# Two small B and C loads, and the scaling and transposing that use them, moved ahead of the last quarter of the input weight

## The chip, the cores and the metric

The kernel runs on one core of one Trainium2 chip. The metric is the device time of one execution in microseconds (us). A core has five engines that run their own instruction streams in order: PE multiplies matrices, DVE, ACT and POOL work on vectors, and SP issues the transfers (DMAs) between the device memory and the core. An engine that meets an instruction whose input isn't there stands, and everything behind it in its stream stands too.

## What is computed

A state-space layer (Mamba2-SSD) over 4 batches, 8 heads and 768 positions, followed by a two-layer perceptron with a tanh GELU over its 3072 x 256 result.

```
for c in range(24):                       # reference: chunks of 32 positions
    cum = cumsum(log a);  L = exp(cum_i - cum_j) * causal
    y_intra = ((C B^T) * L) x
    y_inter = (C state) * exp(cum)
    state = exp(sum log a) * state + sum_j B_j x_j * decay_from_j
h = y.reshape(3072, 256) @ w_in           # w_in 256 x 2048
out = gelu_tanh(h) @ w_out                # w_out 2048 x 256
```

## The kernel before

The kernel takes chunks of Q = 128 positions, six for each batch, 24 in all, and treats two chunks with all 8 heads as a unit u (12 units, 0 to 11). Instead of the exponentials of differences it scales B by a running product of a (`rt0`, `rt`) and C by its reciprocal (`pt0`, `pt`), so that the decay between two positions is a product of the two; a triangle `tri` does the causal part.

Each piece of work is a step: a name, an engine and a function. What order the steps are recorded in, and so in which order each engine gets its instructions, stands written out by hand in the string ORDERED (line 17). An engine's stream is the steps of ORDERED that run on it, in that order; `:A`, `:D` or `:P` behind a name puts a step on ACT, DVE or POOL in place of its usual engine. The framework adds the waits that the data and the buffers need.

```
for w in ORDERED.split():
    ...
        name, _, e = w.partition(":")
        s = steps[name]
        s.eng, s.pre = e or s.eng, int(n or 0)
        s.fn()
```

The steps that the change and the prediction speak of are these.

- Loads on SP: load_wi.q (L192) is quarter q of w_in, 512 KB, 0 to 3. load_bc1.1 and load_bc1.0 (L156) are C and B of chunks 4 and 5 of the first batch, 128 KB each, in pieces of 128 bytes. load_wo.q (L196) is a quarter of w_out, load_x.u (L177, two transfers) x of a unit, load_bc.b.1 and load_bc.b.0 (L170) C and B of batch b.
- wi.q.k and wo.q.k (L339 on POOL, L337 on ACT, L341 on DVE) cast the halves of such a quarter to bf16.
- tp2 (L364) and recip1 (L397) make on DVE the scales for chunks 4 and 5. mul1.0 and mul1.1 (L459, POOL) scale B and C with them. T1.0 and T1.1 (L467, PE) transpose the results into the PSUM banks ga and gb. bh1 and ce1.0, ce1.1 (L478) copy them out. N1 (L487, PE) transposes B back, and bn1 copies that. tp6 (L364) and recip.b (L404) make the scales of the later batches, pe (L408, L409, DVE), pp (L415, PE) and pend (a copy) the decay at the ends of chunks.
- For unit u: G.u (L618, PE) is C B^T into ga and gb; M.u.0 and M.u.1 (L628, DVE) are the masked products from ga and gb; D.u (L651, PE) is the update of the state; S.c.. (L699) and SP.c (L706) carry the state on DVE; Y.u (L673 and L682, PE) is the layer's output, and yev.u copies it to xm as bf16. For units 0 and 1 x is already in the core and XX, XD and xn spread it; from unit 2 on castx.u casts it.
- s1.u.i (L732, PE, i = 0 to 7) multiplies two of the 16 column blocks of w_in with xm into one of the two PSUM buffers hp; gelu.u.i (L736, ACT) empties it. s1.u.4 and s1.u.5 use quarter 2 of w_in, s1.u.6 and s1.u.7 quarter 3. s2.c.q (L750, PE) multiplies with quarter q of w_out; oev.c copies the result out and store.c writes it.

The buffers hp are shared: D.u and pp take one as well, so a matmul into hp also waits until the copy or the gelu of the one but last user is done.

Of the kernel before, what the change touches and what calls it, by code (L numbers as in the profile page):

```python
# [19 lines left out]
recip0 c_m16 mulc.0 ~51 tw.1 ew.1.1:A mulc.1 tw.2 mulb c_sub c_unp c_ends ~4 tw.0 peq ew.0.2 ew.0.1  # L20
load_wi.1 ew.0.0:A ew.1.2 c_par ~4 G.0 x4.1 ew.1.0 x4.0:D M.0.0 ~4 ppq GE.2 GE.3 pendq XX.0 ME.2
XD.0 xn.1 ME.3 xn.0:D load_wi.2 SP.0 ~17 Y.0 wi.0.1:A wi.0.0:A S.0.0 clip R S.0.1 yev.0.0.2 wi.1.1
XX.1 XD.1 wi.1.0 tp2 wi.2.1 xn.2 s1.0.0 G.1 S.1.0 s1.0.1 xn.3 gelu.0.0 gelu.0.1 s1.0.2 gelu.0.2
M.1.1 wi.2.0 M.1.0 s1.0.3 gelu.0.3 s1.0.4 s1.0.5 recip1 S.1.1 gelu.0.4 gelu.0.5 SP.1 load_wi.3
wi.3.1 wi.3.0 load_bc1.1 s1.0.6 load_bc1.0 mul1.0:P SP.2 pe mul1.1:P T1.0 bh1:D tp6 Y.1 gelu.0.6 pp
load_wo.0 pend:D yev.1.0.2 T1.1 N1 wo.0.0 s1.0.7 load_x.2 ce1.1:D castx.2.None ce1.0:D recip.1
s1.1.0 bn1 SP.3 gelu.0.7 wo.0.1 G.2 D.2 gelu.1.0 S.2.0 s1.1.1 gelu.1.1 s2.0.0.0.o s1.1.2 gelu.1.2
s1.1.3 load_bc.1.1 SP.4 load_bc.1.0 M.2.1 M.2.0 gelu.1.3 load_wo.1 s2.0.1.0.o mul.1.0 s1.1.4
mul.1.1:P recip.2 load_x.3 gelu.1.4 wo.1.0 s1.1.5 wo.1.1 Y.2 gelu.1.5 castx.3.None s1.1.6 yev.2.0.2
T.1.0 s1.1.7 gelu.1.6 load_wo.2 E.1.0 T.1.1 s1.2.0 N.1 gelu.1.7 gelu.2.0 E.1.1 bn.1:D s1.2.1 F.1  # L30
s2.0.0.1.o wo.2.0 wo.2.1:D s1.2.2 gelu.2.1 s2.0.1.1.o D.3 G.3 S.3.0 gelu.2.2 s1.2.3 gelu.2.3 S.3.1
M.3.0 M.3.1 load_wo.3 load_x.4 wo.3.0:A s2.0.0.2.o s2.0.1.2.o wo.3.1 SP.6 s1.2.4 s1.2.5 castx.4.None
s2.0.0.3.o s2.0.1.3.o gelu.2.4 gelu.2.5 oev.0:D s1.2.6 Y.3 oev.1 yev.3.0.2:D s2.1.0.0.o s2.1.0.1.o
s2.1.0.2.o gelu.2.6 s2.1.0.3.o s1.2.7 S.4.0 oev.2 recip.3 S.4.1 s1.3.0 s2.1.1.0.o M.4.1 s2.1.1.1.o
gelu.3.0 s2.1.1.2.o gelu.2.7 s2.1.1.3.o s1.3.1 s1.3.2 gelu.3.1 gelu.3.2 oev.3:D s2.2.0.0.o
s2.2.0.1.o s1.3.3 gelu.3.3 s2.2.0.2.o load_bc.2.1 load_bc.2.0 s2.2.0.3.o mul.2.1:P s1.3.4 M.4.0
load_x.5 s1.3.5 gelu.3.4 mul.2.0:P castx.5.None:D SP.7 oev.4:D SP.8 SP.9 s2.2.1.0.o s2.2.1.1.o
gelu.3.5 s2.2.1.2.o s1.3.6 s2.2.1.3.o gelu.3.6 Y.4 load_wr.2.1 s1.3.7 oev.5:D s2.3.0.0.o yev.4.0.2
load_x.6 load_wr.2.0 S.5.0 gelu.3.7 s1.4.0 s2.3.0.1.o M.5.0 load_tr.2.1 gelu.4.0 SP.10 M.5.1 s1.4.1
s2.3.0.2.o castx.6.None s1.4.2 load_bn.2 gelu.4.1 load_tr.2.0 s1.4.3 store.0 s2.3.0.3.o gelu.4.2  # L40
# [961 lines left out]
```

## Time and profile before

| | |
|---|---|
| median of 3 runs | 117.01 us (116.45 to 117.2) |
| the profiled execution | 116.76 us |
| its span in the profile | 115.0 us |
| busy share of PE, DVE, ACT, POOL | 94%, 59%, 61%, 23% |
| matmuls of s1 (L732) | 384, 53.4 us busy, 273 ns each |
| gelu (L736) | 96, 54.3 us busy, 596 ns each |
| moved by DMA | 16.00 MB in 43103 packets |

Times in the profile count from the start of the span. A row of the timeline gives start, duration, engine, line, operation and tiles, how many instructions are taken together, and in brackets the engine's idle time before and what ended it. For transfers the duration is that of SP's issue, and the time to landing stands in the rows of the DMA view. A matmul's duration includes its way through the array: two of 273 ns can start 109 ns apart, so eight of one row take about 0.9 us of PE.

### The profile page before, as it was taken

To read this page: it belongs to the slowest core of one execution; us is meant where nothing else is said; L and a number is where in the kernel's file an instruction comes from. 1 tells how busy PE (TensorE), PEld (TensorE's weight loads), DVE (VectorE), ACT (ScalarE), POOL (GpSimd) and SP (SyncE) were. 2 spreads that over 40 slices of the span, in tenths; PEclk is the share of its full clock that TensorE was granted. 3 is DMA by queue.
4 is the path that set the end of the run, shared out by engine and by line. 5 is a ranking of instruction groups with operands and counts; after the bars stand their busy time and mean duration, and the time that the engine had idled before them with its cause. 6 is when DMAs were issued, how large, how long until landed. Compare 5 with 4: busy or idle time off the path is not lost.

```text
span 115.0 us, 3377 instructions
## 1 busy us (share of the span) xinstructions
PE 108.1 (94%) x1421; PEld 91.7 (80%) x1421; DVE 68.0 (59%) x136; ACT 70.0 (61%) x133; POOL 25.9 (23%) x54
## 2 busy tenths in 40 slices
PE   6979888999999999999999999999999999999990
PEld 2235566888879997989989899889898898999970
DVE  6889998989974755969448491186750851010100
ACT  3159687687654455747675876456495576758620
POOL 7636856806439020201120030000000000000000
PEclk9999999999999999999999999999999999999999
DMA  0999979979994779997556922350003020001113
GB/s 24 231 309 336 332 212 191 317 132 321 215 238 101 141 177 203 196 272 175 88 131 150 209 62 85 111 86 0 0 9 134 0 71 26 0 0 55 42 62 120
DMA packets 43103, 16.00 MB, mean 139 GB/s; under 512 B 36688, under 2 KB 41552, under 8 KB 43088
## 3 DMA queue, kind: packets, MB, share of 16 engines
q1 hardware_dynamic: 42896, 15.70, 55.3%
q8 instruction: 11, 0.18, 0.7%
q10 hardware_dynamic: 192, 0.09, 0.3%
q14 instruction: 4, 0.03, 0.1%
HBM read 11.07 MB, written 3.93 MB: 130 GB/s over the span
## 4 chain that ended last, share of the span: by engine, by line
PE 82%; DVE 5%; DMA 4%; SPq 3%; issue 2%; ACT 2%; DVEq 0%
PE hp L732 35%; PE o_ps L750 34%; DMA x_t<-in_x_dram 4%; PE yb L750 3%; PE yb L673 3%; PE ga L618 2%; PE yb L682 2%; DVE m L628 1%; DVE sp_new L706 1%; SPq L164 1%; ACT gT L736 1%; SPq L151 1%; SPq L160 1%; DVE rt L364 1%; DVE r_t L354 1%
## 5 line engine op out<-in xcount | busy, mean ns | idle before, releaser
L736 ACT ACTIVATE gT<-hp 128x512 bf16<-128x512 f32 x96 | 54.3, 596 | 28.9 <-PE hp L732 28.6
L732 PE MATMUL hp<-xm,w_in_sb 128*128 128x256 bf16 x384 | 53.4, 273 | 1.1 <-DVE s_new L699 0.5
L750 PE MATMUL o_ps<-w_out_sb,gT 128*128 128x256 bf16 x352 | 46.8, 273 | 0.0
L732 PEld LDWEIGHTS <-w_in_sb 128*128 128x128 bf16 x384 | 41.2, 114 | 4.0 <-issue 2.7
L750 PEld LDWEIGHTS <-gT 128*128 128x128 bf16 x384 | 37.4, 98 | 4.1 <-issue 0.4
L341 DVE COPY o_sb<-o_ps 128x256 f32<-128x256 f32 x12 | 5.1, 425 | 26.9 <-PE o_ps L750 26.9
L628 DVE TENSOR_TENSOR m<-ga,tri 128x1024 bf16<-128x1024 f32 x12 | 14.6, 1216 | 0.0
L628 DVE TENSOR_TENSOR m<-gb,tri 128x1024 bf16<-128x1024 f32 x11 | 13.4, 1216 | 0.0
L339 POOL CAST x<-x_t 128x512 bf16<-128x512 f32 x8 | 6.0, 756 | 28.1 <-DMA x_t<-in_x_dram 24.4
L706 DVE SCALAR_TENSOR_TENSOR sp_new<-s_new,pend,bmask 128x256 bf16<-128x256 f32 x17 | 8.0, 483 | 0.1
L699 DVE SCALAR_TENSOR_TENSOR s_new<-s_new,pend,hp 128x64 f32<-128x64 f32 x13 | 3.5, 272 | 7.4 <-PE hp L651 7.3
L720 PE MATMUL yb<-wz 128*128 128x512 bf16 (+2 forms) x21 | 6.6, 455 | 1.1 <-DVE warm L226 1.1
L337 ACT ACTIVATE o_sb<-o_ps 128x256 f32<-128x256 f32 x10 | 3.8, 383 | 5.1 <-PE o_ps L750 3.8
L682 PE MATMUL yb<-m,x 128*32 128x128 bf16 x192 | 6.1, 220 | 0.0
L337 ACT ACTIVATE xm<-yb 128x512 bf16<-128x512 f32 x8 | 4.8, 596 | 1.3 <-PE hp L651 0.7
L720 PEld LDWEIGHTS <-wz 128*128 128x128 bf16 x21 | 2.3, 116 | 4.1 <-issue 2.1
L673 PE MATMUL yb<-ce,sp_new 128*32 128x128 bf16 x160 | 5.3, 221 | 0.0
L339 POOL CAST w_out_sb<-wf 128x512 bf16<-128x512 f32 x6 | 4.1, 692 | 4.7 <-DMA wf<-in_moe_w_out_dram 4.7
L618 PE MATMUL ga<-ce,bh 32*128 32x256 bf16 x48 | 4.7, 273 | 0.3 <-DVE par L289 0.3
L618 PE MATMUL gb<-ce,bh 32*128 32x256 bf16 x48 | 4.7, 273 | 0.0
L750 PE MATMUL yb<-w_out_sb,gT 128*128 128x256 bf16 x32 | 4.5, 273 | 0.0
L682 PEld LDWEIGHTS <-x 128*32 128x32 bf16 x192 | 3.7, 96 | 0.9 <-issue 0.9
(114 smaller groups left out, 75.0 us busy)
## 6 DMA issues: line engine op xcount, KB each, us to landing
out_dram<-o_sb SPq DMA_DIRECT2D x24, 128.0 KB, 2.0
x_t<-in_x_dram SPq DMA_DIRECT2D x20, 128.0 KB, 3.9
wf<-in_moe_w_in_dram SPq DMA_DIRECT2D x4, 512.0 KB, 7.0
wf<-in_moe_w_out_dram SPq DMA_DIRECT2D x4, 512.0 KB, 7.1
bc_t<-in_C_dram SPq DMA_DIRECT2D x3, 384.0 KB, 4.7
bc_t<-in_B_dram SPq DMA_DIRECT2D x3, 384.0 KB, 5.7
scr<-bc SPq DMA_DIRECT2D x4, 192.0 KB, 2.3
x_t<-in_x_dram SPq DMA_DIRECT2D x1, 512.0 KB, 4.4
```

What stands on the lines that cost most here:

```text
L337: nc.scalar.activation(o, i, AF.Copy)
L339: nc.gpsimd.tensor_copy(out=o, in_=i)
L341: nc.vector.tensor_copy(out=o, in_=i)
L618: nc.tensor.matmul(out=gbank(g)[:, 256 * k:256 * k + 256], lhsT=bh_of(2 * u + k)[gs], rhs=ce_of(2 * u + k)[gs], start=True, stop=True, til ...
L628: nc.vector.tensor_tensor(out=m_of(u)[:, 2 * i:2 * i + 2].rearrange("p g k e t -> p (g k e) t"), in0=gx[i].rearrange("p g (k t) -> p (g k) ...
L673: nc.tensor.matmul(out=y4[32 * j:32 * j + 32, k, w], lhsT=sp[:, 32 * h:32 * h + 32], rhs=ce_of(gc)[:, h % 2], start=first(j), stop=False, ...
L682: nc.tensor.matmul(out=y4[32 * j:32 * j + 32, k, w], lhsT=X16[u][:, k, 32 * h:32 * h + 32], rhs=m[:, h // 2, h % 2, :], start=first(j), st ...
L706: nc.vector.scalar_tensor_tensor(out=sp_new.rearrange("p (g d) -> p g d", g=4), in0=(XN[0][:, H * D:H * D + 64] if gc == 0 else state[("s" ...
L720: nc.tensor.matmul(out=t[:, 0:m * 128], lhsT=wz, rhs=w3.to_broadcast([128, m, 128]), start=True, stop=True, skip_group_check=True)
L732: nc.tensor.matmul(out=hp[:, j * T:(j + 1) * T], lhsT=w_in_k[:, w, q, k], rhs=xm[:, w, u * T:(u + 1) * T], start=(w == 0), stop=(w == 1))
L736: nc.scalar.activation(gts[u][:, 2 * i:2 * i + 2], hps.pop((u, i)).rearrange("p (j t) -> p j t", j=2), AF.Gelu_apprx_tanh)
L750: nc.tensor.matmul(out=ops[gc], lhsT=gts[u][:, fi, k * Q:(k + 1) * Q], rhs=w_out_sb[:, fi, :], start=(fi == 0 and (u > 0 or k == 0)), stop ...
```

## The change

Only the string ORDERED is changed; no function is touched. In SP's stream load_bc1.0 and load_bc1.1, B now ahead of C, come in front of load_wi.3 in place of behind it. On POOL mul1.0 comes in front of the two casts of quarter 3, and mul1.1 stays behind them. On PE T1.0 comes between s1.0.3 and s1.0.4; Y.1 and pp come in front of s1.0.6; T1.1 and N1 come between s1.0.6 and s1.0.7; s2.0.0.0 comes behind s1.1.2. On DVE the two state products SP.1 and SP.2 are spread between M.1.0 and M.1.1, which change places, as M.2.0 and M.2.1 do. bh1 and pend move from DVE to ACT, and yev.1 from ACT to DVE. From gelu.1.7 on the string is as before.

The diff, cut to the lines that order these steps:

```diff
-XX.1 XD.1 wi.1.0 tp2 wi.2.1 xn.2 s1.0.0 G.1 S.1.0 s1.0.1 xn.3 gelu.0.0 gelu.0.1 s1.0.2 gelu.0.2
-M.1.1 wi.2.0 M.1.0 s1.0.3 gelu.0.3 s1.0.4 s1.0.5 recip1 S.1.1 gelu.0.4 gelu.0.5 SP.1 load_wi.3
-wi.3.1 wi.3.0 load_bc1.1 s1.0.6 load_bc1.0 mul1.0:P SP.2 pe mul1.1:P T1.0 bh1:D tp6 Y.1 gelu.0.6 pp
-load_wo.0 pend:D yev.1.0.2 T1.1 N1 wo.0.0 s1.0.7 load_x.2 ce1.1:D castx.2.None ce1.0:D recip.1
-s1.1.0 bn1 SP.3 gelu.0.7 wo.0.1 G.2 D.2 gelu.1.0 S.2.0 s1.1.1 gelu.1.1 s2.0.0.0.o s1.1.2 gelu.1.2
-s1.1.3 load_bc.1.1 SP.4 load_bc.1.0 M.2.1 M.2.0 gelu.1.3 load_wo.1 s2.0.1.0.o mul.1.0 s1.1.4
...
+XX.1 XD.1 xn.2 tp2 S.1.0 s1.0.0 G.1 SP.1 load_bc1.0 s1.0.1 wi.1.0 xn.3 M.1.0 gelu.0.0 s1.0.2
+gelu.0.1 gelu.0.2 s1.0.3 SP.2 M.1.1 wi.2.1 wi.2.0 mul1.0:P recip1 gelu.0.3 S.1.1 load_bc1.1
+load_wi.3 T1.0 wi.3.1 s1.0.4 load_wo.0 load_x.2 load_bc.1.1 gelu.0.4 s1.0.5 Y.1 pe gelu.0.5 pp
+wi.3.0 s1.0.6 mul1.1:P T1.1 bh1 tp6 yev.1.0.2:D ce1.1:D N1 pend gelu.0.6 bn1 ce1.0:D load_bc.1.0
+s1.0.7 wo.0.0 s1.1.0 G.2 load_wo.1 gelu.0.7 castx.2.None gelu.1.0 recip.1 SP.3 wo.0.1 D.2 S.2.0
+s1.1.1 M.2.0 s1.1.2 gelu.1.1 s2.0.0.0.o s1.1.3 SP.4 gelu.1.2 M.2.1 s2.0.1.0.o gelu.1.3 s1.1.4 s1.1.5
...
```

More of the change, by code (lines that the diff above doesn't have):

```diff
@@ L28 @@
-s1.1.3 load_bc.1.1 SP.4 load_bc.1.0 M.2.1 M.2.0 gelu.1.3 load_wo.1 s2.0.1.0.o mul.1.0 s1.1.4
[L29 to L37, printed above, removed]
+XX.1 XD.1 xn.2 tp2 S.1.0 s1.0.0 G.1 SP.1 load_bc1.0 s1.0.1 wi.1.0 xn.3 M.1.0 gelu.0.0 s1.0.2
+gelu.0.1 gelu.0.2 s1.0.3 SP.2 M.1.1 wi.2.1 wi.2.0 mul1.0:P recip1 gelu.0.3 S.1.1 load_bc1.1
@@ new lines @@
+load_wi.3 T1.0 wi.3.1 s1.0.4 load_wo.0 load_x.2 load_bc.1.1 gelu.0.4 s1.0.5 Y.1 pe gelu.0.5 pp
+wi.3.0 s1.0.6 mul1.1:P T1.1 bh1 tp6 yev.1.0.2:D ce1.1:D N1 pend gelu.0.6 bn1 ce1.0:D load_bc.1.0
+s1.0.7 wo.0.0 s1.1.0 G.2 load_wo.1 gelu.0.7 castx.2.None gelu.1.0 recip.1 SP.3 wo.0.1 D.2 S.2.0
+s1.1.1 M.2.0 s1.1.2 gelu.1.1 s2.0.0.0.o s1.1.3 SP.4 gelu.1.2 M.2.1 s2.0.1.0.o gelu.1.3 s1.1.4 s1.1.5
+mul.1.0 gelu.1.4 mul.1.1:P recip.2 wo.1.0 wo.1.1 load_x.3 Y.2 s1.1.6 T.1.0 E.1.0 castx.3.None
+gelu.1.5 yev.2.0.2 gelu.1.6 s1.1.7 T.1.1 s1.2.0 N.1 load_wo.2 gelu.1.7 gelu.2.0 E.1.1 bn.1:D s1.2.1
@@ new lines @@
+F.1 s2.0.0.1.o wo.2.0 wo.2.1:D s1.2.2 gelu.2.1 s2.0.1.1.o D.3 G.3 S.3.0 gelu.2.2 s1.2.3 gelu.2.3
+S.3.1 M.3.0 M.3.1 load_wo.3 load_x.4 wo.3.0:A s2.0.0.2.o s2.0.1.2.o wo.3.1 SP.6 s1.2.4 s1.2.5
+castx.4.None s2.0.0.3.o s2.0.1.3.o gelu.2.4 gelu.2.5 oev.0:D s1.2.6 Y.3 oev.1 yev.3.0.2:D s2.1.0.0.o
+s2.1.0.1.o s2.1.0.2.o gelu.2.6 s2.1.0.3.o s1.2.7 S.4.0 oev.2 recip.3 S.4.1 s1.3.0 s2.1.1.0.o M.4.1
+s2.1.1.1.o gelu.3.0 s2.1.1.2.o gelu.2.7 s2.1.1.3.o s1.3.1 s1.3.2 gelu.3.1 gelu.3.2 oev.3:D
+s2.2.0.0.o s2.2.0.1.o s1.3.3 gelu.3.3 s2.2.0.2.o load_bc.2.1 load_bc.2.0 s2.2.0.3.o mul.2.1:P s1.3.4
@@ L38 @@
+M.4.0 load_x.5 s1.3.5 gelu.3.4 mul.2.0:P castx.5.None:D SP.7 oev.4:D SP.8 SP.9 s2.2.1.0.o s2.2.1.1.o
 gelu.3.5 s2.2.1.2.o s1.3.6 s2.2.1.3.o gelu.3.6 Y.4 load_wr.2.1 s1.3.7 oev.5:D s2.3.0.0.o yev.4.0.2
```

## The prediction, as made before the changed kernel ran

> **What bounds the kernel now.** I read the page's first part, then windows over the stretch that the change touches, then PE's waits.
>
> ```profile
> span 115.0 us, 3377 instructions
> PE 108.1 (94%) x1421; PEld 91.7 (80%) x1421; DVE 68.0 (59%) x136; ACT 70.0 (61%) x133; POOL 25.9 (23%) x54
> ...
> 12.00:24.00 12.00, 10.54 (x167) 8.40 (x169) 11.44 (x28) 8.80 (x18) 8.11 (x12) 1.00 1.04 255
> 12.40:20.70 8.30, 7.00 (x96) 5.29 (x97) 7.81 (x22) 6.53 (x13) 5.84 (x11) 1.00 0.99 232
> 60.00:90.00 30.00, 30.00 (x415) 26.79 (x414) 16.25 (x28) 19.40 (x37) 0.86 (x1) 1.00 0.34 84
> ...
> PE hp L732 <- DVE s_new L699: 0.5, 2, 0.3
> PE hp L732 <- ACT gT L736: 0.4, 2, 0.2
> PE ga L467 <- DVE pe L409: 0.4, 1, 0.4
> ```
>
> In a window row the first number after the bounds is its length, then come busy PE, PEld, DVE, ACT and POOL, the granted clock, the DMA share and GB/s. From 60 to 90 us PE has no idle time. From 12.4 to 20.7 us it is idle for 1.30 us, and DVE, busy for 11.44 of the 12 us from 12 to 24, is nearly the second bound there. PE's work is the same before and after, so the change is worth what it moves the point at which PE becomes unbroken. I take s1.1.1, now at 20.70, as that point: the same instructions stand ahead of it in both orders.
>
> The loads, then POOL:
>
> ```profile
> 6.52 0.56 SPq L192 DMA_DIRECT2D wf<-in_moe_w_in_dram  x1
> 7.12 0.47 SPq L156 DMA_DIRECT2D bcf<-in_C_dram  x1
> 7.63 3.38 SPq L156 DMA_DIRECT2D bcf<-in_B_dram  x1
> 11.06 3.26 SPq L196 DMA_DIRECT2D wf<-in_moe_w_out_dram  x1
> ...
> DMA to landing us min/median/max: 8.1/8.1/8.1
> ...
> bcf<-in_C_dram SPq DMA_DIRECT2D x1, 128.0 KB, 9.5
> bcf<-in_B_dram SPq DMA_DIRECT2D x1, 128.0 KB, 9.2
> wf<-in_moe_w_out_dram SPq DMA_DIRECT2D x1, 512.0 KB, 7.3
> ...
> 11.87 2.52 POOL L339 CAST w_in_sb<-wf 128x512 bf16<-128x512 f32 x4 [0.94 <-DMA wf<-in_moe_w_in_dram]
> 14.66 1.17 POOL L339 CAST w_in_sb<-wf 128x512 bf16<-128x512 f32 x2 [0.27 <-DMA wf<-in_moe_w_in_dram]
> 16.99 0.62 POOL L459 TENSOR_TENSOR bc0s<-bcf,rt 128x256 bf16<-128x256 f32 x1 [1.16 <-DVE pe L408]
> 17.57 0.62 POOL L459 TENSOR_TENSOR bc0s<-bcf,pt 128x256 bf16<-128x256 f32 x1
> 19.68 0.62 POOL L339 CAST x<-x_t 128x512 bf16<-128x512 f32 x1 [0.68 <-DMA x_t<-in_x_dram]
> ```
>
> The landing row of 8.1 is that of the last w_in quarter (q3): it lands at 6.52 + 8.1 = 14.6, C at 7.12 + 9.5 = 16.6, B at 7.63 + 9.2 = 16.8. POOL's idle 1.16 us before 16.99 is put down to pe, which mul1.0 doesn't read; B's landing is what it waited for.
>
> **The change part by part.** The instructions of PE and their number stay; what moves is order, and bh1 and pend (DVE to ACT) and yev.1 (ACT to DVE).
>
> ```profile
> 13.66 1.03 PE L732 MATMUL hp<-xm,w_in_sb 128*128 128x256 bf16 x8 [0.31 <-DVE s_new L699]
> 14.94 1.09 PE L732 MATMUL hp<-xm,w_in_sb 128*128 128x256 bf16 x8 [0.25 <-ACT gT L736]
> 16.23 1.09 PE L732 MATMUL hp<-xm,w_in_sb 128*128 128x256 bf16 x8 [0.20 <-ACT gT L736]
> 17.67 0.29 PE L467 MATMUL ga<-ident,bc0s 128*128 128x128 bf16 x2 [0.36 <-DVE pe L409]
> 18.45 0.42 PE L415 MATMUL hp<-pe,selp 128*128 128x48 f32 x2
> 18.93 1.04 PE L732 MATMUL hp<-xm,w_in_sb 128*128 128x256 bf16 x8
> 20.35 0.21 PE L651 MATMUL hp<-x,bn 128*32 128x64 bf16 x4
> 20.70 0.60 PE L732 MATMUL hp<-xm,w_in_sb 128*128 128x256 bf16 x4
> ...
> 13.53 1.22 DVE L628 TENSOR_TENSOR m<-gb,tri 128x1024 bf16<-128x1024 f32 x1
> 16.06 0.87 DVE L706 SCALAR_TENSOR_TENSOR sp_new<-s_new,pendq,bmask 128x256 bf16<-128x256 f32 x2
> 17.04 0.64 DVE L409 TENSOR_TENSOR pe<-pe,m 128x48 f32<-128x48 f32 x1
> 18.34 0.52 DVE L364 STREAM_TRANSPOSE rt<-r_t 128x192 f32<-128x192 f32 x1
> 19.07 0.87 DVE L478 TENSOR_SCALAR ce<-gb,par 128x256 bf16<-128x256 bf16 x2
> 33.40 0.69 DVE L341 CAST xm<-yb 128x512 bf16<-128x512 f32 x1 [0.55 <-PE hp L651]
> ...
> 16.86 1.09 ACT L736 ACTIVATE gT<-hp 128x512 bf16<-128x512 f32 x2 [0.20 <-PE hp L732]
> 19.13 0.38 ACT L337 ACTIVATE bn<-ga 128x256 bf16<-128x256 bf16 x1
> 19.57 1.08 ACT L736 ACTIVATE gT<-hp 128x512 bf16<-128x512 f32 x2
> ```
>
> *B and mul1.0.* B takes q3's place in SP's queue with a quarter of its bytes, so it lands by 14.6. POOL is in its casts until 11.87 + 2.52 = 14.39 anyway. mul1.0 then ends by 14.6 + 0.62 = 15.2.
>
> *T1.0.* It now stands behind s1.0.3, the first half of the pair at 14.94; eight matmuls take about 0.87 (four follow each other in 0.44), so PE reaches it at 15.38. It waits for M.1.0 to free ga too: 13.53 + half of the 0.87 for SP.1 + 1.22 = 15.2. Neither is late, and its 0.29 falls into a stretch in which PE waits for gelu anyway (a pair every 1.28). Cost nothing; without that cover 0.29, and s1.0.4 and s1.0.5 are queued behind it.
>
> *Y.1 and pp.* Y.1 comes after s1.0.5, at 16.23 + 0.44 = 16.67 in place of about 17.9. Its last input, M.1.1, is ready by 13.53 + 0.87 + 2 x 1.22 = 16.84. It takes some 0.5 (T1.0 and Y.1 fill 17.67 to 18.45), so PE is at pp by 17.3. But pp needs pe, and DVE does the same instructions between 13.53 and 17.04 in another order: pe is ready at 17.04 + 0.64 = 17.68 as now. PE waits 0.4, with s1.0.6 queued behind, and leaves pp by about 18.0. Here the lead of 1.2 us is given back, for the first time.
>
> *s1.0.6 and q3.* s1.0.6 needs both casts of q3, which is now loaded behind B and C. Early bound of its landing: 14.6 plus 262 kB at the 255 GB/s of the 12 to 24 us row, 15.6. Late bound: the three loads are the same bytes together, and the last of them lands at 16.8 now. I take 16.8, since the tail of this group is what POOL measurably waited for. The casts end at 16.9 + 1.17 = 18.1, and s1.0.6 starts at 18.15, against 18.0 with the early bound.
>
> A rule bears on this choice.
>
> ```profile
> q8 instruction: 1, 0.02, 6.0%
> ...
> 15.00:15.50 0.50, 0.50 (x5) 0.45 (x5) 0.50 (x1) 0.38 (x1) 0.50 (x2) 1.00 0.58 113
> ```
>
> Between 14 and 15 us an instruction packet is moved beside the loads (first row); by 15.0 to 15.5 the DMA engines are only 58% busy, and still C and B land at 16.6 and 16.8. The Trainium skill, "DMA: Bandwidth & Descriptors", section "Why a DMA increments its semaphore by 16 and not by 1", says that a load on 16 engines counts as landed only when the slowest has posted its share. By that rule whichever load is on a held-up engine at 14 to 15 us is late, and that would now be q3 (sum as with 16.8); if the tail belonged to the small loads alone, the sum would be as with 15.6.
>
> *mul1.1, T1.1, N1.* mul1.1 comes behind q3's casts: 18.1 + 0.62 = 18.7. T1.1, N1 and s1.0.7 follow s1.0.6 (18.6) at 18.75; from T1.1 to the first s1 pass about 0.25 (18.45 to 18.93 holds pp too), so s1.0.7 is at 19.0 to 19.2. ce1 starts on DVE some 0.3 after T1.1, 19.05 against 19.07 now.
>
> *The work that changes engine.* yev.1 on DVE (0.69) comes behind tp6 (0.52): 17.68 + 0.52 + 0.69 = 18.9. That is in front of ce1's start, so it is hidden, and s1.1.0 (about 19.6) has its xm. On ACT, bh1 and pend's two copies (at most 0.38 each, by the row of bn) run from 17.5 to 18.6, where ACT waits for s1.0.6 anyway. But gelu.0.6, whose gelu ran in the pair at 16.86, is now behind pend: an s1 delivers 0.64 after its start (18.93 to 19.57 now), so s1.0.6 at 18.8; gelu.0.6 to 19.4, bn1 to 19.75, gelu.0.7 and gelu.1.0 (1.08) to 20.85. Now the same pair ends at 20.65 and s1.1.1 starts at 20.70; it will start at 20.9. With q3 early the chain gives 20.75.
>
> *What stays.* x of u2 is cast at 19.68 in both orders (the bytes ahead of it are the same), so D.2 stays at about 20.4. s2.0.0.0 goes behind s1.1.2, which lets its w_out cast be later: no cost.
>
> **Sum.** 20.9 - 20.70 = +0.2 (early bound +0.05) on the profiled execution's own 116.76 us: 116.96. That execution lies 0.25 under the 117.01 of the runs, so I forecast 117.1, no change, with 116.7 to 117.5 for this case.
>
> **The rivals.**
>
> *q3 inherits the stuck place (slower).* SP's issue of B lasts 3.38 us and that of the next load 3.26: SP stands while the queue is full of small packets. q3 is now what comes behind B and C. If it fares as w_out's first quarter does in that place, it lands at 11.06 + 7.3 = 18.4. Every later step of the sum moves with it: 1.6 us past 16.8, so 116.96 + 1.6 = 118.6. It decides from a landing after about 16.7 (casts over after pp), one for one. For it: the rows above. Against it: behind B and C q3 needs no early issue, only one before they drain. Half of the price, 117.8, is as possible.
>
> *DVE's idle time closes (faster).* If T1.0's early turn also takes away the waits of DVE and ACT behind it, the most that can come is DVE's idle 12.00 - 11.44 = 0.56 between 12 and 24: 116.2; half of it gives 116.5. For it: B's wait is real, 1.16 us of POOL. Against it: pe's time doesn't move.
>
> *B still lands late (the change doesn't do what it says).* If B's tail hangs on the instruction packet and not on its place, mul1.0 ends at 16.8 + 0.62 = 17.5, PE stands at T1.0 from 15.4 with all of s1.0.4, Y.1 and pp behind it, and s1.1.1 moves by what T1.0 is late less the slack found above: 2.1 - 0.4 = 1.7, or 118.5.
>
> **How the numbers follow.** Forecast 0.56, stuck place 0.24, DVE's idle time 0.14, B late 0.06. Range 116.3 to 118.4: it leaves out the dearest part of the two slow cases and the bottom of the fast one. One per cent, 1.17 us, is about what a measurement of this kernel can tell from no change. Faster by over that needs more than DVE's whole idle time: 0.06, for what I overlook. Slower (over 118.2): 0.17 of the stuck place, 0.05 of B late, 0.02 of the forecast: 0.24. Within: 0.70.
>
> **What would show it.** Right: POOL's mul1.0 directly behind the casts at 14.4 to 14.7, T1.0 near 15.4, Y.1 near 16.7, PE waiting for pe before pp at 17.7, POOL idle until q3 at 15.6 to 16.9, s1.1.1 at 20.7 to 20.9. Wrong: q3 landing past 17.5, mul1.0 past 15.5, or PE idle time after 21 us that isn't there now.

## The result, and the profile after

In 22 runs of each kernel the changed one takes 117.89 us (median) and the one before 117.40. The ratio of the changed kernel to the one before is 1.006, with a 95% interval of 1.0033 to 1.0088: no difference of 1%, but a small loss, some 0.7 us by the ratio and 0.49 between the two medians. The ratios here and below leave out the executions that took over 1.5% longer than the fastest of their kernel: two of these 22 of the changed kernel, five of e3's twelve (four of 119.1 to 120.0 us and one of 379 us), and at most one of each other variant.

In the first profile of the changed kernel the granted clock from 12 to 24 us is 0.89, and the first load of x came about 1 us late, ahead of everything that the change touches. The reading below therefore goes by a second execution of the same kernel at a clock of 1.00 (e6 among the experiments, 118.16 us). The first part of its page, three of its windows (behind them one of the kernel before), and two rows of its waits:

```profile
span 116.5 us, 3376 instructions
PE 109.0 (94%) x1421; PEld 91.9 (79%) x1421; DVE 67.3 (58%) x134; ACT 69.9 (60%) x135; POOL 25.6 (22%) x54
```

```profile
12.00:24.00 12.00, 9.80 (x152) 7.75 (x150) 10.52 (x24) 8.25 (x19) 8.01 (x12) 1.00 0.95 233
60.00:90.00 30.00, 30.00 (x380) 27.16 (x380) 16.41 (x28) 19.34 (x37) 0.61 (x1) 1.00 0.37 94
13.00:14.00 1.00, 0.69 (x12) 0.52 (x13) 0.95 (x4) 0.63 (x2) 0.80 (x3) 1.00 0.62 112
...
13.00:14.00 1.00, 0.69 (x13) 0.52 (x13) 0.95 (x4) 0.66 (x2) 0.85 (x3) 1.00 1.23 275
```

```profile
PE hp L732 <- POOL w_in_sb L339: 0.9, 1, 0.9
PE yb L682 <- DVE m L628: 0.5, 1, 0.5
```

PE still has no idle time from 60 to 90 us. From 12 to 24 us it is busy for 9.80 us, where it was 10.54 before, and two waits are new: 0.9 us for q3's casts on POOL, and 0.5 us for DVE's masked product at Y.2. From 13 to 14 us its transfers moved 112 GB/s, where those of the kernel before (the last window) moved 275. The timeline of the same execution shows the first one come about. The rows are SP's issues, then POOL, PE and DVE.

```profile
6.50 0.37 SPq L156 DMA_DIRECT2D bcf<-in_B_dram  x1
6.91 2.14 SPq L156 DMA_DIRECT2D bcf<-in_C_dram  x1
9.09 3.92 SPq L192 DMA_DIRECT2D wf<-in_moe_w_in_dram  x1
...
14.62 0.62 POOL L459 TENSOR_TENSOR bc0s<-bcf,rt 128x256 bf16<-128x256 f32 x1
17.65 1.17 POOL L339 CAST w_in_sb<-wf 128x512 bf16<-128x512 f32 x2 [2.41 <-DMA wf<-in_moe_w_in_dram]
20.21 0.61 POOL L339 CAST x<-x_t 128x512 bf16<-128x512 f32 x1 [0.26 <-DMA x_t<-in_x_dram]
22.49 1.49 POOL L499 TENSOR_TENSOR bc<-bc_t,pt 128x768 bf16<-128x768 f32 x1 [1.11 <-DMA bc_t<-in_C_dram]
...
15.37 0.27 PE L467 MATMUL ga<-ident,bc0s 128*128 128x128 bf16 x2
16.73 0.30 PE L673 MATMUL yb<-ce,sp_new 128*32 128x128 bf16 x8
17.57 0.39 PE L415 MATMUL hp<-pe,selp 128*128 128x48 f32 x2 [0.21 <-ACT gT L736]
18.87 0.63 PE L732 MATMUL hp<-xm,w_in_sb 128*128 128x256 bf16 x4 [0.91 <-POOL w_in_sb L339]
19.45 0.29 PE L467 MATMUL gb<-ident,bc0s 128*128 128x128 bf16 x2
21.47 1.03 PE L732 MATMUL hp<-xm,w_in_sb 128*128 128x256 bf16 x8 [0.21 <-ACT gT L736]
...
15.24 0.47 DVE L706 SCALAR_TENSOR_TENSOR sp_new<-s_new,pendq,bmask 128x256 bf16<-128x256 f32 x1
17.03 0.15 DVE L408 TENSOR_TENSOR pe<-ac,r_t 128x3 f32<-128x3 f32 x1
17.22 0.21 DVE L409 TENSOR_TENSOR pe<-pe,m 128x48 f32<-128x48 f32 x1
22.90 1.36 DVE L706 SCALAR_TENSOR_TENSOR sp_new<-s_new,pend,bmask 128x256 bf16<-128x256 f32 x1
```

The lead is there: mul1.0 at 14.62 in place of 16.99, T1.0 at 15.37 in place of 17.67, Y.1 at 16.73. But SP stands for 3.92 us with the issue of q3, and q3 lands last: 9.09 + 8.5 = 17.6 by the DMA view of that issue.

```profile
wf<-in_moe_w_in_dram SPq DMA_DIRECT2D x1, 512.0 KB, 8.5
```

Its casts run from 17.65 to 18.82, s1.0.6 starts at 18.87, and s1.1.1 at 21.47 in place of 20.70. So 0.77 of the 1.5 us by which the two spans differ stands ahead of s1.1.1; most of the rest is Y.2's wait behind it (0.5). This execution is 0.27 us above the kernel's median.

Of the three profiles of the changed kernel this is the only one in which PE waits for q3's casts. In the first one and in e1's they end later still, at 19.5 and 19.8, but PE, late by x and at a lower clock, reaches s1.0.6 only at 19.97 and 20.81.

### The profile page after: what moved, and what is told of

It is laid out like the page before. It is cut to its first block, busy times and chain, and to the rows that moved or that the text cites. A ratio compares the mean times of both kernels' runs of the same rounds, so it can differ in the third digit from the quotient of the medians.

```text
span 117.0 us, 3376 instructions
## 1 busy us (share of the span) xinstructions
PE 109.6 (94%) x1421; PEld 92.1 (79%) x1421; DVE 68.9 (59%) x134; ACT 70.1 (60%) x135; POOL 25.2 (22%) x54
## 4 chain that ended last, share of the span: by engine, by line
PE 83%; DMA 5%; DVE 4%; ACT 3%; SPq 2%; issue 1%
PE hp L732 34%; PE o_ps L750 33%; DMA x_t<-in_x_dram 5%; PE yb L750 3%; PE yb L682 3%; PE yb L673 2%; PE ga L618 2%; DVE m L628 2%; PE yb L720 1%; ACT gT L736 1%; PE hp L586 1%; SPq L151 1%; SPq L164 1%; DVE sp_new L706 1%; SPq L160 1%
## 5 line engine op out<-in xcount | busy, mean ns | idle before, releaser
L628 DVE TENSOR_TENSOR m<-ga,tri 128x1024 bf16<-128x1024 f32 x12 | 14.6, 1215 | 0.0
L628 DVE TENSOR_TENSOR m<-gb,tri 128x1024 bf16<-128x1024 f32 x11 | 13.4, 1215 | 0.0
L706 DVE SCALAR_TENSOR_TENSOR sp_new<-s_new,pend,bmask 128x256 bf16<-128x256 f32 x17 | 8.6, 522 | 0.1
L720 PE MATMUL yb<-wz 128*128 128x512 bf16 (+2 forms) x21 | 7.4, 498 | 1.1 <-DVE warm L226 1.1
L682 PE MATMUL yb<-m,x 128*32 128x128 bf16 x192 | 6.6, 227 | 0.0
L337 ACT ACTIVATE xm<-yb 128x512 bf16<-128x512 f32 x7 | 4.2, 597 | 1.5 <-PE yb L682 0.7
```

Of the source, the lines that this page charges most:

```text
L337: nc.scalar.activation(o, i, AF.Copy)
L628: nc.vector.tensor_tensor(out=m_of(u)[:, 2 * i:2 * i + 2].rearrange("p g k e t -> p (g k e) t"), in0=gx[i].rearrange("p g (k t) -> p (g k) ...
L682: nc.tensor.matmul(out=y4[32 * j:32 * j + 32, k, w], lhsT=X16[u][:, k, 32 * h:32 * h + 32], rhs=m[:, h // 2, h % 2, :], start=first(j), st ...
L706: nc.vector.scalar_tensor_tensor(out=sp_new.rearrange("p (g d) -> p g d", g=4), in0=(XN[0][:, H * D:H * D + 64] if gc == 0 else state[("s" ...
L720: nc.tensor.matmul(out=t[:, 0:m * 128], lhsT=wz, rhs=w3.to_broadcast([128, m, 128]), start=True, stop=True, skip_group_check=True)
```

## The experiments

All variants differ only in the hand-written order. A ratio is to the kernel before, measured alongside, with its 95% interval.

**e1 and e6: the changed kernel again.**

> The changed kernel itself, once more, for a profile in which its first x load isn't late. Theory A (the forecast's): w_in's last quarter (q3) lands at about 16.8, PE leaves pp at 18.0, s1.0.6 starts at about 18.15 and s1.1.1 at 20.9; ratio to before 1.002. Theory B (the stuck place): SP stands with C's issue and then with q3's, q3 lands at 17.7 to 18.4 in a run whose s1.0.0 starts near 12.4, s1.0.6 starts behind q3's casts at 18.9 to 19.6, s1.1.1 at 21.4 to 22.3; ratio 1.006 to 1.014.

> The changed kernel a third time, for a profile in which s1.0.0 starts near 12.4 to 12.7. Theory B (stuck place): SP stands for over 3 us with C and again with q3, the DMA share falls under 0.6 between 14 and 16, q3 lands at 17.4 to 18.4, s1.0.6 is released by q3's casts and starts at 18.7 to 19.6, s1.1.1 at 21.3 to 22.2. Theory C alone: q3 lands by 17 and s1.0.6 is released by pp at 18.5, s1.1.1 at 21.1.

e1 measured 1.0057 (1.0019 to 1.0096), 117.78 us, against 1.002 by theory A and 1.006 by theory B; the loss is real and small. Its profile has the late first x as well. e6 is the profile shown above. q3's landing at 17.6, s1.0.6 behind its casts at 18.87 and s1.1.1 at 21.47 are as theory B had them; but SP stood only 2.14 with C, and the busy share of the DMA engines fell between 13 and 14 us (0.62), not between 14 and 16.

**e2: the order of the loads alone.**

```diff
-SP.1 load_wi.3 wi.3.1 wi.3.0 load_bc1.1 s1.0.6 load_bc1.0 mul1.0:P
+SP.1 load_bc1.0 load_bc1.1 load_wi.3 wi.3.1 wi.3.0 s1.0.6 mul1.0:P
```

> The kernel before with its loads alone in the new order (B, C, q3 on SP); PE, DVE, ACT and POOL keep their order. It prices q3's lateness where nothing is gained by B's earliness, since both casts of q3 stand in front of mul1.0 and s1.0.6 in front of T1.0. Theory A: q3 lands at 16.8, its casts end at 18.1 in place of 15.8, s1.0.6 starts at 18.15 in place of 16.7; T1.0 at about 18.75 in place of 17.67; ratio 1.008 to 1.010. Theory B: q3 lands at 17.7 to 18.4, T1.0 at 19.7 to 20.3; ratio 1.017 to 1.023.

Measured 1.0199 (1.0144 to 1.0253), as theory B had it; the profiled execution, at a clock of 1.00, took 118.78 us, 1.016 times the 116.91 of the kernel before. SP, PE and POOL in its timeline:

```profile
9.09 4.54 SPq L192 DMA_DIRECT2D wf<-in_moe_w_in_dram  x1
...
19.13 0.63 PE L732 MATMUL hp<-xm,w_in_sb 128*128 128x256 bf16 x4 [2.38 <-POOL w_in_sb L339]
...
17.90 1.17 POOL L339 CAST w_in_sb<-wf 128x512 bf16<-128x512 f32 x2 [2.77 <-DMA wf<-in_moe_w_in_dram]
19.04 0.63 POOL L459 TENSOR_TENSOR bc0s<-bcf,rt 128x256 bf16<-128x256 f32 x1
```

q3 lands at 17.8, against 17.6 in e6. With the engines in the old order mul1.0 also stands behind its casts, so everything is late by q3: s1.0.6 waits 2.38 us. The place behind B and C makes q3 late by itself, and the new order on the engines hides most of it.

**e3: the order of the engines alone.**

```diff
-SP.1 load_bc1.0 ... S.1.1 load_bc1.1 load_wi.3 T1.0
+SP.1 load_wi.3 load_bc1.1 load_bc1.0 ... S.1.1 T1.0
```

> The changed kernel with the loads in the order of before (q3, C, B on SP); the engines keep the new order, so mul1.0 stands in front of q3's casts and waits for B. It shows whether B's landing hangs on its place. Both theories: B lands at about 16.8 as before, mul1.0 ends at 17.5, PE stands at T1.0 from 15.4 to 17.5; s1.1.1 near 22.4; ratio 1.013 to 1.017. If B lands earlier than 16 here, the tail of 16.8 belonged to that one profile and both theories lose their footing.

Measured 1.0047 (1.0005 to 1.0089), cheaper than expected, by the seven executions that are not left out.

```profile
17.33 0.29 PE L467 MATMUL ga<-ident,bc0s 128*128 128x128 bf16 x2 [0.89 <-POOL bc0s L459]
...
16.65 0.62 POOL L459 TENSOR_TENSOR bc0s<-bcf,rt 128x256 bf16<-128x256 f32 x1 [1.28 <-DMA bcf<-in_B_dram]
```

B lands at 16.5, late as before the change (16.8), and T1.0 waits for it; but the profile also began s1.0 late, at 13.31 in place of 12.42 (the first x again), and so the wait shows only 0.89 us. By the ratio late B costs this order some 0.5%, not over 1%.

**e4: B, then q3, then C.** C isn't needed before mul1.1, which stands behind q3's casts anyway.

```diff
-S.1.1 load_bc1.1 load_wi.3 T1.0
+S.1.1 load_wi.3 load_bc1.1 T1.0
```

> The changed kernel with C alone behind q3 again (B, q3, C on SP): C is first read by mul1.1, which stands behind q3's casts in any case. Theory A: q3 lands by 15.6 to 16, s1.0.6 starts at 18.0 behind pp, C lands at 16.8 and isn't late for mul1.1 at 17.3 to 18; s1.1.1 at 20.75; ratio 1.000, so 0.002 under the changed kernel. Theory B: q3 leaves the stuck place to C, lands by 15.6 to 16 and s1.0.6 starts at 18.0; ratio 1.000 too, but 0.006 to 0.014 under the changed kernel.

Measured 1.0014 (0.9988 to 1.0041). SP, POOL, DVE and PE:

```profile
6.42 0.37 SPq L156 DMA_DIRECT2D bcf<-in_B_dram  x1
6.83 2.08 SPq L192 DMA_DIRECT2D wf<-in_moe_w_in_dram  x1
8.95 0.98 SPq L156 DMA_DIRECT2D bcf<-in_C_dram  x1
9.97 3.13 SPq L196 DMA_DIRECT2D wf<-in_moe_w_out_dram  x1
...
15.22 1.36 POOL L339 CAST w_in_sb<-wf 128x512 bf16<-128x512 f32 x2
17.48 0.62 POOL L459 TENSOR_TENSOR bc0s<-bcf,pt 128x256 bf16<-128x256 f32 x1 [0.90 <-DVE pt L397]
...
15.20 0.90 DVE L706 SCALAR_TENSOR_TENSOR sp_new<-s_new,pendq,bmask 128x256 bf16<-128x256 f32 x1
17.61 0.55 DVE L409 TENSOR_TENSOR pe<-pe,m 128x48 f32<-128x48 f32 x1
...
18.31 0.39 PE L415 MATMUL hp<-pe,selp 128*128 128x48 f32 x2 [0.55 <-DVE pe L409]
18.54 0.60 PE L732 MATMUL hp<-xm,w_in_sb 128*128 128x256 bf16 x4
```

The long stand of SP has gone on to w_out's quarter (3.13), which nobody needs early; q3 lands at 15.2, and most of the loss is gone: 1.0014, where the changed kernel measured alongside (e1) has 1.0057, and all twelve executions lie between 116.83 and 117.36 us. s1.0.6 is at 18.54, not at the 18.0 that was expected, because the wait moves to pe. pe is late because SP.2 takes 0.90 beside q3's casts (0.47 in e6, where POOL was idle) and L409 0.55 beside mul1.1 (0.21 in e6). POOL's casts take 1.36 in place of 1.17. It looks as if DVE and POOL hold each other up; e5 and e9 look into that.

**e5: e4 with SP.1 and SP.2 behind S.1.1, out of the casts' way.**

```diff
-G.1 SP.1 load_bc1.0 ... s1.0.3 SP.2 M.1.1 ... S.1.1 load_wi.3
+G.1 load_bc1.0 ... s1.0.3 M.1.1 ... S.1.1 SP.1 SP.2 load_wi.3
```

> The kernel of e4 (B, q3, C) with SP.1 and SP.2 on DVE behind S.1.1 again, as before the change. In e4's profile each of them overlaps casts of POOL and takes 0.62 and 0.90 us in place of 0.48, the casts beside them 1.36 a pair in place of 1.17, and pe is ready at 18.15 in place of 17.68. Theory C (the two engines hold each other up): behind S.1.1 POOL is between its casts and mul1.1, the two take 0.87 together, pe is ready at 17.7, pp starts at 17.75, s1.0.6 at 18.0, s1.1.1 at 20.75; ratio to before 1.000, 0.003 under e4. Rival (their length in e4 has another cause, the order or the data): pe stays at 18.1 and the ratio that of e4, 1.001 to 1.002.

Measured 1.0039 (1.0006 to 1.0073): missed. DVE, POOL and PE:

```profile
16.17 0.88 DVE L706 SCALAR_TENSOR_TENSOR sp_new<-s_new,pendq,bmask 128x256 bf16<-128x256 f32 x2
16.96 0.60 DVE L408 TENSOR_TENSOR pe<-ac,r_t 128x3 f32<-128x3 f32 x1
17.59 0.56 DVE L409 TENSOR_TENSOR pe<-pe,m 128x48 f32<-128x48 f32 x1
...
16.77 1.34 POOL L339 CAST w_in_sb<-wf 128x512 bf16<-128x512 f32 x2 [1.72 <-DMA wf<-in_moe_w_in_dram]
...
18.31 0.39 PE L415 MATMUL hp<-pe,selp 128*128 128x48 f32 x2 [0.80 <-DVE pe L409]
```

The state products have their 0.88 for two again, but in this execution q3 came at 16.7 and its casts met pe: L408 took 0.60 where it takes 0.15. pp is at 18.31, to the hundredth where e4 has it. By the same reading the contention wasn't removed, it met other instructions.

**e9: e4 with q3's casts on ACT.** It leaves POOL idle between mul1.0 and mul1.1, with DVE's stream unchanged.

```diff
-T1.0 wi.3.1 s1.0.4 ... gelu.0.5 pp wi.3.0 s1.0.6
+T1.0 s1.0.4 ... gelu.0.5 wi.3.1:A wi.3.0:A pp s1.0.6
```

> The order of e4 (B, q3, C), but q3's two casts stand on ACT, behind gelu.0.5, in place of POOL: POOL has nothing to do between mul1.0 and mul1.1, while DVE's stream is the same. Theory (DVE and POOL lengthen each other's instructions when both work from the core's memory at once): SP.1 and SP.2 take at most 0.5 us each (0.62 and 0.90 in e4), pe (L408 and L409) at most 0.4 in all (0.15 + 0.55 in e8), so pe is ready by 17.4 and PE leaves the wait ahead of pp by 17.8 in place of 18.31. The two casts on ACT end at about 18.6, so s1.0.6 is at about 18.65, and the time is 0.1 to 0.6 us over e4's. Rival (SP is long because DMA writes or PE's work stand beside it, not POOL's): SP.2 stays at 0.8 to 0.9 and pp at about 18.3.

One execution, 117.39 us (before: 116.88, median of 11). DVE, then POOL, then PE:

```profile
13.50 0.90 DVE L706 SCALAR_TENSOR_TENSOR sp_new<-s_new,pendq,bmask 128x256 bf16<-128x256 f32 x1
14.33 1.21 DVE L628 TENSOR_TENSOR m<-ga,tri 128x1024 bf16<-128x1024 f32 x1
15.46 0.47 DVE L706 SCALAR_TENSOR_TENSOR sp_new<-s_new,pendq,bmask 128x256 bf16<-128x256 f32 x1
17.25 0.15 DVE L408 TENSOR_TENSOR pe<-ac,r_t 128x3 f32<-128x3 f32 x1
17.44 0.55 DVE L409 TENSOR_TENSOR pe<-pe,m 128x48 f32<-128x48 f32 x1
...
13.52 1.37 POOL L339 CAST w_in_sb<-wf 128x512 bf16<-128x512 f32 x2 [0.22 <-DMA wf<-in_moe_w_in_dram]
17.30 0.62 POOL L459 TENSOR_TENSOR bc0s<-bcf,pt 128x256 bf16<-128x256 f32 x1 [1.84 <-DVE pt L397]
...
18.13 0.39 PE L415 MATMUL hp<-pe,selp 128*128 128x48 f32 x2 [0.55 <-DVE pe L409]
```

The rows of SP.1, SP.2, L408 and L409 go by whether POOL works at that moment. SP.2 and L408, now alone, take 0.47 and 0.15; SP.1, still beside q2's casts, and L409, still beside mul1.1, take 0.90 and 0.55. I had overlooked those two neighbours, so pp came at 18.13 and not by 17.8; but the rival, by which SP.2 stays at 0.8 to 0.9 with POOL idle, is refuted by this execution. L409 ends at 17.99, 0.07 after mul1.1 (17.92), and in e4 0.06 after it (18.16 and 18.10): it waits until POOL's instruction is over. M.1.0 (L628), which reads one of its two inputs from PSUM, keeps its 1.21 beside the casts.

**e7, e8 and e10: versions that use this.** e7 takes before's order with B, q3, C loaded early and T1.0 ahead of s1.0.4; e8 is e4 with pp behind s1.0.6; e10 is e7 with s1.0.7 ahead of pp.

```diff
 e7, on before
+S.1.0 load_bc1.0 load_wi.3 load_bc1.1 s1.0.1 ... gelu.0.2 M.1.0 M.1.1 ... gelu.0.3 mul1.0:P T1.0 s1.0.4 ... gelu.0.5 bh1 SP.1
 e8, on e4
-gelu.0.5 pp wi.3.0 s1.0.6 mul1.1:P ... bh1 tp6 ... pend gelu.0.6
+gelu.0.5 wi.3.0 s1.0.6 pp mul1.1:P ... bh1 gelu.0.6 tp6 ... pend
 e10, on e7
-gelu.0.6 pp load_wo.0 pend:D ... wo.0.0 s1.0.7 ... SP.3 gelu.0.7
+gelu.0.6 s1.0.7 pp load_wo.0 gelu.0.7 pend:D ... wo.0.0 ... SP.3
```

> A version built from what the runs showed: the kernel before with B, q3, C on SP, mul1.0 in front of q3's casts, T1.0 in front of s1.0.4, M.1.0 in front of M.1.1 (so that ga is free), and bh1 on ACT behind gelu.0.5. SP.1 and SP.2, s1.0.6 in front of Y.1, pp behind Y.1, pend on DVE and yev.1 on ACT stay as before. Worked out from the rows of before and e4: s1.0.6 at 16.85, Y.1 at 17.3, pp at 17.75, T1.1 and N1 at 18.0, s1.0.7 at 18.3, ce1 at 18.4 to 19.3, G.2 at 19.3, s1.1.1 at 20.0 to 20.3; ratio 0.994 to 0.997. Rival: DVE, busy for 11.4 of 12 us there, gives nothing back and M.2 holds Y.2: ratio 1.000.

> The kernel of e4 with s1.0.6 in front of pp on PE and gelu.0.6 in front of pend on ACT. It tells whether PE's wait for pe at pp (0.55 us in e4) is what the lead of T1.0 and Y.1 goes into. If so: s1.0.6 at about 17.3 to 17.5 in place of 18.54, pp at 18.3, T1.1 then, s1.0.7 at 18.8, s1.1.1 at 20.6 to 20.8; ratio 0.998, 0.003 under e4. Rival (DVE's chain pe, tp6, yev.1, ce1 sets G.2 and gelu.1.0 anyway): s1.1.1 stays at 21.0 to 21.1, ratio that of e4.

> The order of e7, and besides s1.0.7 in front of pp and gelu.0.7 in front of pend and yev.1, so that the last pair of s1.0 is done while pe is still on its way. If s1.1.1 alone decides, it is at 20.0 to 20.2 (20.32 in e7, 20.70 before) and the time is 0.4 to 0.6 us under before: ratio 0.995 to 0.997. Rival (DVE's stream from pend to M.2.0 and M.2.1 is the bound there, so what PE gains ahead of s1.1.1 it loses waiting at Y.2): the span less the start of s1.1.1 grows from 94.4 to 94.7 or more, and the ratio stays at about 0.9985.

e7 measured 0.9985 (0.9951 to 1.0019), s1.1.1 at 20.32; e8 1.0001 (0.997 to 1.0031), s1.1.1 at 20.86; e10 1.0112 (1.0059 to 1.0165), s1.1.1 at 22.20. No version beats the kernel before by what can be measured. e7's s1.1.1 is about where it was expected, but the ratio isn't down at 0.994 to 0.997; e8 lies between what was expected of it (0.998) and e4. e7 is the best; there DVE's SP.1 and SP.2 meet q3's casts and mul1.1, and take 1.54 for the two. e10 missed on the slow side, for a reason that I had not foreseen. PE, DVE, POOL and ACT of e10:

```profile
17.99 0.63 PE L732 MATMUL hp<-xm,w_in_sb 128*128 128x256 bf16 x4 [1.22 <-POOL w_in_sb L339]
20.91 0.60 PE L732 MATMUL hp<-xm,w_in_sb 128*128 128x256 bf16 x4 [0.79 <-ACT xm L337]
...
19.94 0.26 DVE L341 COPY pend<-hp 128x16 f32<-128x16 f32 x2 [1.49 <-PE hp L415]
...
16.58 1.36 POOL L339 CAST w_in_sb<-wf 128x512 bf16<-128x512 f32 x2 [1.03 <-DMA wf<-in_moe_w_in_dram]
...
20.27 0.59 ACT L337 ACTIVATE xm<-yb 128x512 bf16<-128x512 f32 x1
```

With s1.0.7 ahead of pp, pp starts at 19.58; DVE stands 1.49 for it, and yev.1 behind gelu.0.7 on ACT makes s1.1.0 wait 0.79. Besides, q3 came at 16.5 and cost s1.0.6 its 1.22.

## Why the prediction was right and where it was not

**The outcome.** 117.89 lies in the range, and no change of 1% is what was forecast. But 117.1 was too low by 0.8, and 117.89 lies above the 117.5 up to which the forecast's own case went: that it is inside the range is owed to the room left for the slow rivals. Half of the 0.8 is the kernel before, whose median in these runs is 117.40 and not 117.01; the other half is the change, 0.49 between the medians (0.7 by the ratio) where I had worked out 0.2, and one step has most of it. The last addition was off as well: 116.96 and 0.25 make 117.2, not 117.1.

**s1.1.1 as the point that decides: right.** The span less the start of s1.1.1 is 94.3 to 94.6 us in ten of the twelve profiles, whether it starts at 20.32 (e7) or 23.38 (e1). The two others are e6 (95.0) and e10 (94.9).

**B, mul1.0, T1.0, Y.1: right.** 14.62, 15.37 and 16.73 against 14.4 to 14.7, 15.38 and 16.67. The lead of over 2 us at T1.0 is worth nothing at s1.1.1, as worked out.

**pe as now at 17.68: wrong, without effect here.** DVE's instructions are the same, but their durations are not. L409's 0.64 before was no property of L409: mul1.0 stood beside it. With mul1.0 gone pe is ready at 17.43, and what PE waits for before pp is ACT (0.21). pp still ends at 17.96, against 18.0.

**s1.0.6 and q3: the mis-sized term.** I took 16.8 as q3's late bound, because the same bytes ended there before; it landed at 17.6. The 16.8 wasn't the end of the bytes either: before the change fifteen of the sixteen parts of B had landed by 15.59, and one came at 16.85. Nor did the bytes set q3's time, since from 13 to 14 us the DMA engines were busy for only 0.62 of the time. SP did: the load behind both small ones isn't through its issue until 13.0 (e6) and 13.6 (e2), and lands 4.6 and 4.2 us after that. w_out's quarter, in that place before, landed 4.0 us after its issue (14.32, landing 18.36), and 3.0 us in e3. Why SP stands there, whether because the queue is full or for another reason, no row shows. This is the rival of the stuck place, at half of its price: it gave 117.8 for that case, and I gave it the smaller chance; its sign, q3 landing past 17.5, came true. From there all steps are late together: s1.0.6 18.87 for 18.15, T1.1 19.45 for 18.75, s1.1.1 21.47 for 20.9. e4, with one load exchanged, shows that q3's place was the cause: 1.0057 becomes 1.0014.

**The engine with the tail.** The Trainium skill, "DMA: Bandwidth & Descriptors", section "Why a DMA increments its semaphore by 16 and not by 1", was weighed for q3's landing: a load counts only when its slowest engine is done. For e6 it isn't the reason, since half of q3's sixteen parts land after 17.1. In e4 and e5, of one load order, fifteen parts are there by 15.11 and 15.08, and the last lands at 15.16 and 16.71: there the trace agrees, and the time of q3 differs by 1.5 us between executions by it.

**What stays: wrong.** x of u2 was to be cast at 19.68. POOL, free at 19.95, waited 0.26 for x and cast it at 20.21: the same bytes were ahead of it, and it still landed later. D.2 came at 21.04 for 20.4, without a wait of its own, since all of PE was late by then. I named PE idle time after 21 us as a sign of error, and e6 has it: SP.4 takes 1.36 beside POOL's L499 (0.48 before, when L499 started after it), M.2.1 comes late, and Y.2 waits 0.5.

**The other rivals.** Late B did not occur; by e3's ratio it would have cost about 0.5%, not 1.7 us. DVE's idle time did not become a gain: from 12 to 24 us DVE is busy for 10.52 in e6, where it was 11.44, and pe came 0.25 earlier, but PE then stood for q3.

## What to carry to other kernels

When a large load goes behind small-packet loads, cost its landing from the end of its issue on the queue (3.0 to 4.6 us later in these traces), not from the bytes; put behind them the load that nobody needs soon. Reordering DVE against POOL changes durations, so "the same instructions in another order" is no reason for the same end: look at which POOL instruction stands beside each DVE instruction with two inputs in the core's memory. A lead on one engine is worth only what it moves at the point after which the bound engine never stands.

## What the runs showed of the hardware

DVE instructions with both inputs in the core's memory and POOL's casts and products wait for each other for whole instructions: L408 takes 0.15 alone and 0.59 to 0.60 beside a cast, L409 0.21 and 0.51 to 0.64, L706 0.47 and up to 1.36, a pair of casts 1.17 and 1.36. The Trainium skill, "SBUF — State Buffer", section "SBUF: two separate sides", says that such a DVE instruction and a POOL instruction that reads the same memory take a shared port in turn, and that the later one stands until the other is over; the trace agrees, L409's end lying 0.06 to 0.07 us behind POOL's.

One part of sixteen of a load can lag by 0.9 to 1.8 us, and the following loads with it (C and B in the profile before; q3 in e5, e9 and e10; the first x in e1, e3 and the first profile of the changed kernel). It differs between executions of the same order of loads; what causes it stays open, and no run was made on it.
